# Windowed attention on one Trainium2 core: the products with v as four 64x64 quarters in two rounds

## The chip, the cores and the metric

The kernel runs on one NeuronCore of a Trainium2 chip. The metric is the device time of one execution in microseconds (us): 766.04 us for the kernel before (median of 3 runs, 765.94 to 767.62). All tensors are float32.

## What is computed

Attention over a causal window of 128 keys (8 batches, 8 heads, 576 positions, 64 wide), and behind it a maxout layer:

```python
scores = scale * np.matmul(q, k.transpose(0, 1, 3, 2))
...
mask = (rel >= 0) & (rel < window)          # rel = query - key, window = 128
scores = np.where(mask, scores + bias[None], -1000000000.0)
...
attn = attn / (np.sum(attn, axis=-1, keepdims=True) + 1e-09)
return np.matmul(attn, v).astype(np.float32)

h = np.maximum(np.maximum(x @ w1, x @ w2), x @ w3)
return (h @ w_out).astype(np.float32)
```

## The kernel before, in words

**Tasks and blocks.** A task is a batch and a pair of heads: 8 x 4 = 32 tasks. Positions are cut into five blocks of 128 (the last has 64: `rows = [128, 128, 128, 128, 64]`). A step is one block of one task; steps are handled two at a time. For each pair of steps TensorE makes the scores (`products`, L397), VectorE masks and adds the bias (L430, L444), ScalarE takes the exponential (L448) and scales (L472), TensorE transposes the result (`turn`, L481), ScalarE copies it out of PSUM (L489, L495, L498), and GpSimd masks it (L501, L505) into the tiles `pp`. A tile `pp[t, i]` has the 128 keys of block i on the partitions, and for both heads the 128 queries of block i and the 128 of block i + 1, since a key can be seen by queries up to 127 positions later.

**The products with v.** For the 28 tasks of batches 1 to 7 `mix` (L533 to L559) takes a block of 128 keys at a time: for each of the two heads one matmul with `vt[t][:n, i, j * D:(j + 1) * D]` (128 keys x 64) as the weights and the 256 query columns of `pp[t, i]` as the moving operand. The head decides the half of the array's columns and so the half of the partitions of `ps_x` (a PSUM tile of two banks, one buffer). The calls come in two groups per task: blocks 0 and 1, some steps later blocks 2, 3 and 4 (`GROUPS = (1, 4)`). The 576 output columns cross from one bank to the other at column 512, so block 3 is split there. After block 4 ScalarE copies the 576 columns to `xk` (L559). Batch 0 does the same in `mix_first` (L510 to L531), in other groups and with a copy for each. A float32 matmul of the code is two rows in the trace (28 tasks x 12 matmuls x 2 = 672).

**The maxout layer.** `plain_unit` (L722) and `unit` (L760) are 77 units per batch, in fp32r, of 6 or 9 matmuls of 128x128 weights and 288 columns; these products are made by seven products of halves instead of eight. Weights stream from DRAM into a ring of two (L314, issued by GpSimd). Results go through VectorE and ScalarE (L669 to L686, L769), and are cut into two fp32r parts for the next product (L576, L577).

**What sets the order.** Each call is an event with a due time (`at`); units are spread between the attention steps at an even pace. The recorded program is then ordered by a scheduler, up to `fix`, from which on TensorE keeps the program's order (`keep_in_program_order`, through `pe`). In the first stretch idle TensorE time is filled with dummy matmuls (`busy`, L336).

Of the kernel before, what the change touches and what calls it, by code (L numbers as in the profile page):

```python
# [29 lines left out]
def attention_maxout_kernel(  # L30
# [11 lines left out]
    nc = tc.nc  # L42
# [431 lines left out]
    def turn(s):  # L474
        pt = ps_t.tile([P, 2, 2, P], F32, name="pt")
        two = steps[s:s + 2]
        for a, (t, i) in enumerate(two):
            n = rows[i]
            p = pn.pop((t, i))
            for j in range(2):  # L480
                ins = nc.tensor.transpose(out=pt[:, a, j, :n], in_=p[:n, j], identity=ident[:n, :n])  # L481
                pe(ins)
        if idle[0] != "over":
            idle[0] = ins
            busy("t")
# [21 lines left out]
                compare_op=ALU.is_ge, fill=0.0, base=0, channel_multiplier=-1,  # L507
            )

    def mix_first(t, late):  # L510
        b, hp = tasks[t]
        x = ps_x.tile([P, 1024], F32, name="ps_x")
        c0 = FIRST * P if late else 0
        c1 = S if late else FIRST * P
        for i in range(FIRST - late, NB) if late else range(FIRST):
            n = rows[i]
            a, e = max(c0, i * P), min(c1, (i + 2) * P)
            for j in range(2):
                ins = nc.tensor.matmul(  # L519
                    x[j * D:(j + 1) * D, a - c0:e - c0],  # L520
                    lhsT=vt[t][:n, i, j * D:(j + 1) * D],
                    rhs=pp[t, i][:n, j].rearrange("p a b -> p (a b)")[:, a - i * P:e - i * P],
                    start=i == (FIRST - late if late else 0), stop=True, skip_group_check=True,
                )
                pe(ins)
        if idle[0] != "over":
            idle[0] = ins
            busy("x")
        if not late and hp % 2 == 0:
            xk[b, hp // 2] = xk_p.tile([P, 2, S], F32, name=f"xk{hp // 2}")  # L530
        nc.scalar.copy(out=xk[b, hp // 2][:, hp % 2, c0:c1], in_=x[:, :c1 - c0])  # L531

    def mix(t, i):  # L533
        b, hp = tasks[t]
        if i == 0:
            xp[t] = ps_x.tile([P, 1024], F32, name="ps_x")
        x, vv, w = xp[t], vt[t], pp[t, i]
        n = rows[i]
        m = rows[i + 1] if i + 1 < NB else 0
        parts = []  # L540
        c0 = i * P
        if m == 0 or (c0 // 512 != (c0 + P) // 512):
            parts.append((0, n, c0))
            if m:
                parts.append((P, P + m, c0 + P))
        else:
            parts.append((0, P + m, c0))
        for a, e, c in parts:
            for j in range(2):
                pe(nc.tensor.matmul(  # L550
                    x[j * D:(j + 1) * D, c:c + e - a],
                    lhsT=vv[:n, i, j * D:(j + 1) * D],
                    rhs=w[:n, j].rearrange("p a b -> p (a b)")[:, a:e],
                    start=i == 0 or (c % 512 == 0 and a == P), stop=True, skip_group_check=True,
                ))
        if i == NB - 1:
            if hp % 2 == 0:
                xk[b, hp // 2] = xk_p.tile([P, 2, S], F32, name=f"xk{hp // 2}")
            nc.scalar.copy(out=xk[b, hp // 2][:, hp % 2], in_=x[:, :S])  # L559

# [138 lines left out]
    def plain_unit(v):  # L699
# [19 lines left out]
            part_of["plain"] = ps_m.tile([P, 512], F32, name=f"ps_m{v // 2 % 3}")[:, :C]  # L719
        ps = part_of["plain"]  # L720
        for m, (lt, rt) in enumerate(pairs):
            pe(nc.tensor.matmul(  # L722
                ps, lhsT=lt, rhs=rt, start=m == 0 and c == 0, stop=m == len(pairs) - 1, skip_group_check=True,
            ))
        if (i, j, c) == (1, 1, 1):
            used.add((g, "plain"))
        if c:
# [2 lines left out]
    def unit(u):  # L730
# [26 lines left out]
            part_of[n, k] = ps_m.tile([P, 512], F32, name=f"ps_m{u % 3}")[:, :C]  # L757
        ps = part_of[n, {2: 0, 5: 0, 6: 0, 3: 1}.get(k, k)]
        for i, (lt, rt) in enumerate(pairs):
            pe(nc.tensor.matmul(  # L760
                ps, lhsT=lt, rhs=rt, start=i == 0 and k in (0, 1, 4), stop=i == len(pairs) - 1,
                skip_group_check=True,
            ))
        if g < 9:
            used.add((at, k))
        stream()
# [21 lines left out]
    for t, (b, hp) in enumerate(tasks):  # L788
        for i in range(NB):
# [27 lines left out]
                at(s + 1.3, normalise, t, i)  # L817
            if b == 0:
                if i in (FIRST - 1, NB - 1):
                    at(c + LAG_X0 + 0.001, mix_first, t, i == NB - 1)  # L820
                continue
            e = t * NB + next(min(e + 1, NB - 1) for e in GROUPS if e >= i)
            at(e - e % 2 + shift[b] + LAG_X + 0.001, mix, t, i)

    ready = [n_steps * (b + 1) - 2 + LAG_X + 0.05 + shift[b] for b in range(B)]
    ready[0] += LAG_X0 - LAG_X
# [80 lines left out]
```

## Time and profile before

| what | value |
|---|---|
| median of three runs | 766.04 us |
| span of the profiled execution | 765.8 us |
| TensorE matmul busy | 754.3 us (98%) |
| VectorE busy | 561.6 us (73%) |
| ScalarE busy | 499.6 us (65%) |
| GpSimd busy | 174.5 us (23%) |
| products with v, batches 1 to 7 (L550) | 672 matmuls, 65.3 us busy |

The profiled execution's own time is its span, 765.8 us; it lies 0.2 us under the median of the runs. PE is TensorE's matmul side, PEld its weight loads, DVE VectorE, ACT ScalarE, POOL GpSimd. A busy time is the union of the instructions' durations, and a matmul's duration runs on for a while after its last column has gone in, so a busy PE is not a full one. A group is written out<-in with its shapes (rows x columns of the array that the instruction uses, 128\*64 or 64\*64, then the output), the count, busy us and the mean ns of one.

### The profile page before, as it was taken

How to read it: one execution, taken by the hardware profiler on the slowest of the kernel's cores; microseconds unless marked ns; L12 is line 12 of the kernel's file. 1: busy time of each engine (PE TensorE's matmuls, PEld its weight loads, DVE VectorE, ACT ScalarE, POOL GpSimd, SP SyncE). 2: the span in 40 equal slices, each digit the busy share in tenths (PEclk: the TensorE clock that was granted, in tenths of full speed). 3: DMA queues.
4: the chain of work that ended last, by engine and by line, in shares of the span. 5: the costliest groups of instructions: out<-in, count | busy, mean ns of one | idle time of the engine just before them, and what ended most of it. 6: DMA issues, size and time to landing. Idle time of an engine off the chain costs nothing.

```text
span 765.8 us, 18225 instructions
## 1 busy us (share of the span) xinstructions
PE 754.3 (98%) x6417; PEld 670.4 (88%) x6417; DVE 561.6 (73%) x1921; ACT 499.6 (65%) x1674; POOL 174.5 (23%) x380
## 2 busy tenths in 40 slices
PE   9999999999999999999999999999999999999997
PEld 4588888988899998989899988999989988999987
DVE  6989997799996577947678477774769566673762
ACT  5867887687886576756677566766677566642431
POOL 2421231111141222212222122312322123311100
PEclk9999999999999999999999999999999999999999
DMA  8789975888994698737976488745887369776651
GB/s 301 262 305 320 331 266 163 293 275 298 336 308 158 197 322 281 253 128 235 318 245 213 158 299 278 260 156 204 291 292 270 106 232 307 262 225 204 226 178 63
DMA packets 56539, 187.97 MB, mean 245 GB/s; under 512 B 6144, under 2 KB 17920, under 8 KB 49664
## 3 DMA queue, kind: packets, MB, share of 16 engines
q0 software_dynamic: 16272, 99.10, 39.1%
q1 hardware_dynamic: 40032, 87.64, 33.0%
q8 instruction: 51, 0.84, 0.4%
q14 instruction: 40, 0.33, 0.1%
q10 hardware_dynamic: 144, 0.07, 0.0%
HBM read 154.53 MB, written 32.24 MB: 244 GB/s over the span
## 4 chain that ended last, share of the span: by engine, by line
PE 73%; DVE 18%; ACT 4%; DMA 2%; issue 2%; SPq 0%; POOL 0%; ACTq 0%; DVEq 0%; POOLq 0%
PE ps_m L760 48%; PE ps_x L550 6%; PE ps_m L722 6%; PE ps_s L397 6%; PE pt L481 4%; DVE hs L577 3%; PE ps_m L336 2%; DVE xs L577 2%; DVE t L683 2%; DVE s L444 2%; ACT p L448 1%; DVE hq L684 1%; DMA hs<-in_w_all 1%; DVE ps_s L430 1%; ACT xs L576 1%
## 5 line engine op out<-in xcount | busy, mean ns | idle before, releaser
L760 PE MATMUL ps_m<-xs,wt 128*128 128x288 f32 x2604 | 365.3, 298 | 3.4 <-DVE t L683 1.5
L760 PEld LDWEIGHTS ps_m<-xs,wt 128*128 128x128 f32 x2604 | 349.9, 188 | 7.2 <-DVE t L683 2.9
L448 ACT ACTIVATE p<-s,st 128x128 f32<-128x128 f32 (+1 forms) x320 | 127.0, 399 | 21.7 <-DVE st L444 21.3
L501 POOL TENSOR_SCALAR_AFFINE_SELECT pp<-pr 128x256 f32<-128x256 f32 (+1 forms) x128 | 56.8, 444 | 357.9 <-ACT pr L498 202.3
L769 ACT COPY t<-ps_m 128x288 f32<-128x288 f32 x231 | 89.5, 393 | 70.8 <-PE ps_m L760 70.1
L760 PE MATMUL ps_m<-hs,ow 128*128 128x288 f32 x882 | 124.0, 298 | 1.6 <-DVE hs L577 0.8
L760 PEld LDWEIGHTS ps_m<-hs,ow 128*128 128x128 f32 x882 | 118.7, 189 | 3.1 <-ACT t L769 1.1
L472 ACT ACTIVATE p<-p,st 128x128 f32<-128x128 f32 (+1 forms) x296 | 103.1, 396 | 21.0 <-DVE st L460 20.8
L314 POOL DMA_DIRECT2D wt<-keep x106 | 56.9, 537 | 191.7 <-PE ps_m L760 184.5
L444 DVE CUSTOM_DVE_ANT_0 s<-ps_s,bias 128x128 f32<-128x128 f32 (+1 forms) x300 | 76.3, 280 | 18.7 <-PE ps_s L397 17.0
L683 DVE TENSOR_TENSOR t<-ps_m,t 128x288 f32<-128x288 f32 x126 | 56.4, 452 | 37.2 <-PE ps_m L760 25.0
L430 DVE COPY_PREDICATED ps_s<-prev,ps_s 128x256 f32<-128x256 uint8 x120 | 50.7, 423 | 40.4 <-PE ps_s L397 39.1
L576 ACT CAST hs<-hq 128x288 fp32r<-128x288 f32 x117 | 48.9, 430 | 31.0 <-DVE hq L684 17.0
L550 PE MATMUL ps_x<-pp,v 128*64 128x256 f32 (+3 forms) x672 | 65.3, 321 | 0.0
L505 POOL TENSOR_SCALAR_AFFINE_SELECT pp<-pr 128x256 f32<-128x256 f32 (+1 forms) x128 | 63.1, 493 | 5.5 <-PE ps_x L519 5.5
L397 PE MATMUL ps_s<-qk 64*64 64x192 f32 (+1 forms) x1052 | 63.1, 323 | 0.4 <-DVE st L444 0.4
L498 ACT COPY pr<-pt 128x256 f32<-128x256 f32 x68 | 20.1, 322 | 65.7 <-PE pt L481 65.7
L448 ACT ACTIVATION_READ_ACCUMULATOR p<-s,st 128x1 f32 (+1 forms) x320 | 61.1, 191 | 0.0
L684 DVE TENSOR_TENSOR hq<-t,hq 128x288 f32<-128x288 f32 x126 | 57.0, 459 | 2.0
L577 DVE TENSOR_TENSOR hs<-hq,hs 128x288 fp32r<-128x288 f32 x117 | 53.5, 463 | 5.7 <-ACT hs L576 5.5
L550 PEld LDWEIGHTS ps_x<-pp,v 128*64 128x64 f32 (+1 forms) x672 | 38.8, 135 | 19.2 <-issue 9.1
L481 PEld LDWEIGHTS pt<-ident,p 128*128 128x128 f32 (+1 forms) x320 | 33.5, 140 | 24.1 <-issue 16.2
(84 smaller groups left out, 858.9 us busy)
## 6 DMA issues: line engine op xcount, KB each, us to landing
wt<-keep POOLq DMA_DIRECT2D x53, 1024.0 KB, 7.4
wt<-keep POOLq DMA_DIRECT2D x53, 768.0 KB, 5.8
qk<-in_qk SPq DMA_DIRECT2D x28, 576.0 KB, 5.4
hs<-in_w_all SPq DMA_DIRECT2D x20, 512.0 KB, 6.0
outT<-t SPq DMA_DIRECT2D x64, 144.0 KB, 1.8
v<-in_v SPq DMA_DIRECT2D x28, 320.0 KB, 5.3
keep<-wt SPq DMA_DIRECT2D x30, 256.0 KB, 3.7
wt<-keep SPq DMA_DIRECT2D x27, 256.0 KB, 4.2
```

Of the source, the lines that this page charges most:

```text
L397: ins = nc.tensor.matmul(ps[j][d:d + D, o:o + k1 - k0], lhsT=qkt[t][j * D:(j + 1) * D, 0, q0:q0 + D], rhs=qkt[t][j * D:(j + 1) * D, 1, k0:k1],
L444: follow(nc.vector.tensor_tensor_reduce(out=s[:n], in0=ps[j][:n, P:2 * P], in1=(bias if i else bias0)[:n, 2 * hp + j, :], scale=-0.125, sc ...
L448: nc.scalar.activation(p[:n, j], s[:n], AF.Exp, bias=st[:n, 0, a, j:j + 1], scale=-1.0, accum_out=st[:n, 1, a, j:j + 1])
L472: nc.scalar.activation(p[:n, j], p[:n, j], AF.Copy, scale=st[:n, 2, a, j:j + 1])
L481: ins = nc.tensor.transpose(out=pt[:, a, j, :n], in_=p[:n, j], identity=ident[:n, :n])
L505: nc.gpsimd.affine_select(out=w[:n, :, 0, :n], in_=r[:n, a, :, :n], pattern=[[0, 2], [1, n]], compare_op=ALU.is_ge, fill=0.0, base=0, chan ...
L550: pe(nc.tensor.matmul(x[j * D:(j + 1) * D, c:c + e - a], lhsT=vv[:n, i, j * D:(j + 1) * D], rhs=w[:n, j].rearrange("p a b -> p (a b)")[:, ...
L577: e.tensor_tensor(out=lo, in0=src, in1=hi.bitcast(F32), op=ALU.subtract)
L683: nc.vector.tensor_tensor(out=s, in0=ps, in1=e, op=ALU.add)
L684: nc.vector.tensor_tensor(out=h, in0=s, in1=h, op=ALU.max)
L760: pe(nc.tensor.matmul(ps, lhsT=lt, rhs=rt, start=i == 0 and k in (0, 1, 4), stop=i == len(pairs) - 1, skip_group_check=True,))
L769: nc.scalar.copy(out=e, in_=ps)
```

## The change

The products with v use quarters of the array: 64 keys x 64 output columns. `quarter` multiplies half r of the keys of a block by chosen query halves, for both heads. With the window of 128, half 0 of a block's keys meets the first and second half of the same block's queries and the first half of the next block's; half 1 meets the second half of the same block's and both halves of the next block's. So 6 of the 8 combinations of a key half and a query half are made, where all 8 were made before. The output of the even query halves lies in the first bank of `ps_x`, that of the odd ones in the second.

In round `near` key half 0 goes with even query halves (first bank) and key half 1 with odd ones (second bank), up to 128 columns each. In round `far` key half 0 goes with the odd half of the same block (second bank) and key half 1 with the even half of the next block (first bank), 64 columns each: the banks have swapped. Between the rounds stands the semaphore `turned`: `near` ends with `drain(fusable=True)` that raises it, and the first matmul of `far` waits for it. `far` is not issued by `mix` but held, and issued by `apart` behind the next scores, transposes or unit. In the built program 60 of the 64 raises sit on the last matmul of `near` and 4 (in batch 0) on a drain instruction of their own; 2 more drains stand ahead of transposes (`fence`). The masking and the tiles `pp` are as before. At the end of a task ScalarE copies the two banks apart, into alternating groups of 64 columns of `xk`: two copies (320 and 256 columns) instead of one of 576. `mix_first` is gone; batch 0 uses `mix` with its own bounds.

```diff
@@ products, turn, plain_unit, unit: after the last matmul
+        apart(ins)
...
+    def quarter(x, t, k, r, parts, e, first):
+        i, w = k, pp[t, k]
+        ks = slice(r * D, (r + 1) * D)
...
+        a, qs, q0 = parts
+        for j in range(2):
+            m = nc.tensor.matmul(
+                x[j * D:(j + 1) * D, q0:q0 + e * D],
+                lhsT=vt[t][ks, i, j * D:(j + 1) * D],
+                rhs=w[ks, j, a:a + e, qs * D:(qs + 1) * D],
+                start=first, stop=True, skip_group_check=True,
+            )
...
+    def turned_by():
+        ins = nc.tensor.drain(fusable=True)
...
+        ins.then_inc(turned, 1)
...
+    def near(x, t, blocks, fresh):
+        last = []
+        for n, (i, cur, nxt) in enumerate(blocks):
+            a, e = (0 if cur else 1), cur + nxt
+            last += quarter(x, t, i, 0, (a, 0, (i + a) * D), e, fresh and n == 0)
+            e = (cur and rows[i] == P) + (nxt and rows[i + 1] == P)
+            if e:
+                last += quarter(x, t, i, 1, (a, 1, 512 + (i + a) * D), e, fresh and n == 0)
+        return last
+
+    def far(x, t, blocks):
+        made = []
+        for i, cur, nxt in blocks:
+            if cur and rows[i] == P:
+                made += quarter(x, t, i, 0, (0, 1, 512 + i * D), 1, False)
+            if nxt:
+                made += quarter(x, t, i, 1, (1, 0, (i + 1) * D), 1, False)
+        return made
+
+    def apart(ins):
...
+            made = far(x, t, blocks)
+            made[0]._wait_ge(turned, turns[0])
...
+                for par in range(2):
+                    ks = [k for k in range(*done) if k % 2 == par]
+                    src = x[:, par * 512 + ks[0] // 2 * D:][:, :len(ks) * D]
+                    nc.scalar.copy(
+                        out=out[:, ks[0]:ks[-1] + 1:2], in_=src.rearrange("p (n d) -> p n d", d=D)
+                    )
...
+    def mix(t, lo, hi, first, done):
...
+        made = near(x, t, blocks[::-1] if not first else blocks, first)
...
+        made.append(turned_by())
...
+        held.append((x, t, blocks, made[-1], done))
...
-            nc.scalar.copy(out=xk[b, hp // 2][:, hp % 2], in_=x[:, :S])
```

How TensorE's rows stand, batch 1, the second group of a task. Ahead of it and behind it stand units of the maxout layer. Before:

```order
L550 MATMUL ps_x<-pp,v 64x256 [waits Pool_49]
L550 MATMUL ps_x<-pp,v 64x256
L550 MATMUL ps_x<-pp,v 64x128 [waits Pool_49]
L550 MATMUL ps_x<-pp,v 64x128
L550 MATMUL ps_x<-pp,v 64x64 [waits Pool_49]
L550 MATMUL ps_x<-pp,v 64x64
L550 MATMUL ps_x<-pp,v 64x64 [waits Pool_49]
L550 MATMUL ps_x<-pp,v 64x64
L397 MATMUL ps_s<-qk 64x128 [waits DMAHW7_49,DVE_49]
L397 MATMUL ps_s<-qk 64x128 x3
L397 MATMUL ps_s<-qk 64x192 x4
L481 MATMUL pt<-ident,p 128x128 [waits PE_49]
```

and in the changed program (L532 is the matmul of `quarter`, L482 the transpose):

```order
L532 MATMUL ps_x<-pp,v 64x64 [waits Pool_49]
L532 MATMUL ps_x<-pp,v 64x64
L532 MATMUL ps_x<-pp,v 64x128 x2
L532 MATMUL ps_x<-pp,v 64x64 x2
L532 MATMUL ps_x<-pp,v 64x128 x4
L397 MATMUL ps_s<-qk 64x128 [waits DMAHW7_49,DVE_49]
L397 MATMUL ps_s<-qk 64x128 x3
L397 MATMUL ps_s<-qk 64x192 x4
L532 MATMUL ps_x<-pp,v 64x64 [waits turned]
L532 MATMUL ps_x<-pp,v 64x64 x7
L482 MATMUL pt<-ident,p 128x128 [waits PE_49]
```

The scores, which stood behind all products with v, now stand between the two rounds; `far` stands between scores and transposes. A first group of a task stands the same way (`near` is 64x128 x8 there, `far` 64x64 x8). At four places of batches 1 to 7 there are no scores between the rounds; the last of them, at the end of batch 7, reads:

```order
L532 MATMUL ps_x<-pp,v 64x128 x4
L820 MATMUL ps_m_11222<-hs,ow_118 128x288 [waits DVE_49]
L820 MATMUL ps_m_11222<-hs,ow_118 128x288 x5
L820 MATMUL ps_m_11222<-hs_11187,ow_118 128x288 [waits DVE_49]
L820 MATMUL ps_m_11222<-hs_11187,ow_118 128x288 [waits Activation_49]
L820 MATMUL ps_m_11222<-hs_11187,ow_118 128x288
L532 MATMUL ps_x<-pp,v 64x64 [waits turned]
L532 MATMUL ps_x<-pp,v 64x64 x7
```

Here a unit of 128x128 weights has come between the two rounds, where before the products of the group stood in one piece; at the three other places it is the four transposes.

## Rows read from the trace of the kernel before

**Rows 1.** The page: span, busy time by engine (share of span, instructions), granted clock in 40 slices.
```profile
span 765.8 us, 18225 instructions
...
PE 754.3 (98%) x6417; PEld 670.4 (88%) x6417; DVE 561.6 (73%) x1921; ACT 499.6 (65%) x1674; POOL 174.5 (23%) x380
...
PEclk9999999999999999999999999999999999999999
```

**Rows 2.** Waits of PE, the largest: waited for, us in total, times, longest us.
```profile
PE ps_m L760 <- DVE t L683: 1.5, 6, 0.6
```

**Rows 3.** The chain that ended last: the page's shares by engine; its first and last L550.
```profile
PE 73%; DVE 18%; ACT 4%; DMA 2%; issue 2%; SPq 0%; POOL 0%; ACTq 0%; DVEq 0%; POOLq 0%
...
80.99 1.01 PE ps_x L550 x8
...
673.18 1.18 PE ps_x L550 x16
```

**Rows 4.** The chain that ended last, 300 to 440 us: start us, us, what.
```profile
303.87 1.01 PE ps_x L550 x8
304.88 0.81 PE ps_s L397 x16
...
308.16 0.40 ACT t L769
...
328.27 5.05 PE ps_m L760 x36
...
342.55 1.12 PE ps_x L550 x14
...
351.26 1.01 PE ps_x L550 x8
```

**Rows 5.** Timeline of PE, a second group (493 us), and scores without a group (70 us).
```profile
493.35 1.19 PE L550 MATMUL ps_x<-pp,v 128*64 128x256 f32 x14
...
494.37 0.23 PE L550 MATMUL ps_x<-pp,v 64*64 64x64 f32 x2
...
495.06 0.66 PE L481 MATMUL pt<-ident,p 128*128 128x128 f32 x4
...
70.25 0.76 PE L397 MATMUL ps_s<-qk 64*64 64x192 f32 x12
70.94 0.66 PE L481 MATMUL pt<-ident,p 128*128 128x128 f32 x4
```

**Rows 6.** Groups with shapes kept apart: xcount | busy us, mean ns | idle before.
```profile
L550 PE MATMUL ps_x<-pp,v 128*64 128x256 f32 x336 | 48.7, 396 | 0.0
...
L550 PE MATMUL ps_x<-pp,v 128*64 128x128 f32 x112 | 10.9, 273 | 0.0
...
L550 PE MATMUL ps_x<-pp,v 128*64 128x64 f32 x112 | 8.0, 220 | 0.0
```

**Rows 7.** L550, then L397 from 303 to 306 us: ns min/median/max; L397 from 304.80 to 304.84.
```profile
L550 PE MATMUL ps_x<-pp,v x8: 379/380/431, 303.8 to 304.5; 128*64 128x256 f32 x8
...
L397 PE MATMUL ps_s<-qk x16: 322/323/374, 304.8 to 305.4; 64*64 64x192 f32 x16
...
304.81 0.39 PE L397 MATMUL ps_s<-qk 64*64 64x192 f32 x4
```

**Rows 8.** ScalarE: the copy of one task on the timeline, and by form (as rows 6).
```profile
494.64 0.64 ACT L559 COPY xk<-ps_x 128x576 f32<-128x576 f32 x1
...
L769 ACT COPY t<-ps_m 128x288 f32<-128x288 f32 x231 | 89.5, 393 | 70.8 <-PE ps_m L760 70.1
```

**Rows 9.** Stretches: us, busy us of PE, PEld, DVE, ACT, POOL, clock, DMA share, GB/s.
```profile
80.00:100.00 20.00, 20.00 (x184) 16.72 (x184) 19.82 (x69) 15.89 (x58) 4.47 (x10) 1.00 0.98 341
100.00:120.00 20.00, 19.65 (x188) 17.30 (x185) 19.77 (x72) 17.41 (x63) 4.08 (x8) 1.00 0.65 221
...
398.00:418.00 20.00, 20.00 (x177) 18.99 (x176) 19.12 (x57) 15.15 (x46) 5.33 (x11) 1.00 0.68 235
```

**Rows 10.** Timeline of PE at 292.5 us: idle time just before, and what ended it.
```profile
292.50 0.53 PE L760 MATMUL ps_m<-xs,wt 128*128 128x288 f32 x2 [0.19 <-DVE t L683]
```

More of the change, by code (lines that the diff above doesn't have):

```diff
@@ L482, in turn @@
                 pe(ins)
+                if not fixed and fence[0] is not None and fence[1] is None:
+                    after(ins, fence[0])
+                    fence[1] = ins
+        apart(ins)
         if idle[0] != "over":
@@ L508, in turn @@
             )
[L510 to L525, printed above, removed]
+    held = []
@@ new lines, in attention_maxout_kernel, with after @@
+    turned = tc.alloc_semaphore("turned")
+    turns = [0]
+    fence = [None, None]
+    def after(ins, first):
+        tc.add_manual_dep(
+            ins.ins, first.ins.name,
+            mybir.DependencyInfo(mybir.DependencyClass.NoSync, mybir.DependencyReason.DATA), reason="order",
+        )
+    def quarter(x, t, k, r, parts, e, first):
+        i, w = k, pp[t, k]
+        ks = slice(r * D, (r + 1) * D)
+        ins = []
+        a, qs, q0 = parts
[6 more added lines that the diff above has]
+            )
+            pe(m)
+            ins.append(m)
+        return ins
@@ new lines, in far @@
+    def far(x, t, blocks):
[7 more added lines that the diff above has]
+    def apart(ins):
+        while held:
+            x, t, blocks, last, done = held.pop(0)
+            if not fixed:
+                after(ins, last)
+            made = far(x, t, blocks)
+            made[0]._wait_ge(turned, turns[0])
+            fence[:] = [None if fixed else made[-1], None]
+            if not fixed:
+                after(made[0], ins)
+                for m, n in zip(made[1:], made):
+                    after(m, n)
+            if done is not None:
+                b, hp = tasks[t]
+                if hp % 2 == 0 and (b, hp // 2) not in xk:
+                    xk[b, hp // 2] = xk_p.tile([P, 2, S], F32, name=f"xk{hp // 2}")
+                out = xk[b, hp // 2][:, hp % 2].rearrange("p (n d) -> p n d", d=D)
+                for par in range(2):
[3 more added lines that the diff above has]
+                        out=out[:, ks[0]:ks[-1] + 1:2], in_=src.rearrange("p (n d) -> p n d", d=D)
+                    )
@@ new lines, in mix @@
+    def mix(t, lo, hi, first, done):
+        if first:
+            xp[t] = ps_x.tile([P, 1024], F32, name="ps_x")
+        x = xp[t]
+        blocks = []
+        for i in range(NB):
+            cur = lo <= i < hi
+            nxt = lo <= i + 1 < hi if tasks[t][0] == 0 else cur and i + 1 < NB
+            if cur or nxt:
+                blocks.append((i, cur, nxt))
+        made = near(x, t, blocks[::-1] if not first else blocks, first)
+        if fence[0] is not None:
+            if fence[1] is None:
+                fence[1] = nc.tensor.drain()
+                after(fence[1], fence[0])
+            after(made[0], fence[1])
+        made.append(turned_by())
+        if not fixed:
+            for m, n in zip(made[1:], made):
+                after(m, n)
@@ L526, in mix_first @@
         if idle[0] != "over":
-            idle[0] = ins
+            idle[0] = made[-1]
             busy("x")
[L529 to L558, printed above, removed]
-            nc.scalar.copy(out=xk[b, hp // 2][:, hp % 2], in_=x[:, :S])
@@ L819, in attention_maxout_kernel @@
                 if i in (FIRST - 1, NB - 1):
-                    at(c + LAG_X0 + 0.001, mix_first, t, i == NB - 1)
+                    late = i == NB - 1
+                    at(
+                        c + LAG_X0 + 0.001, mix, t, FIRST if late else 0, NB if late else FIRST, True,
+                        (2 * FIRST, 9) if late else (0, 2 * FIRST),
+                    )
                 continue
-            e = t * NB + next(min(e + 1, NB - 1) for e in GROUPS if e >= i)
-            at(e - e % 2 + shift[b] + LAG_X + 0.001, mix, t, i)
+            if i in GROUPS:
+                e = t * NB + min(i + 1, NB - 1)
+                lo = GROUPS[0] + 1 if i == NB - 1 else 0
+                at(e - e % 2 + shift[b] + LAG_X + 0.001, mix, t, lo, i + 1, lo == 0, (0, 9) if i == NB - 1 else None)
     ready = [n_steps * (b + 1) - 2 + LAG_X + 0.05 + shift[b] for b in range(B)]
```

15 lines of the change are left out of this document (11 added, 4 removed).

## The prediction, written before the changed kernel ran

> **What bounds the kernel now.** I read the page first. PE is busy for 754.3 of 765.8 us and the granted clock stands at full speed in every slice [rows 1], so the clock is no part of this change. A busy PE need not be the bound; PE's waits tell whether it is. The longest, for VectorE's L683, comes to 1.5 us in the whole span [rows 2]: PE hardly ever waits. The chain that ended last says the same from the other side: 73% of it is PE [rows 3]. The second thing to see is where that chain leaves PE. In a stretch of 90 us it runs through units, products with v (L550), scores and transposes, leaves PE at 308.16 us and comes back at 328.27 us [rows 4]; in between ScalarE and VectorE set the pace, and time that PE saves there is lost. So what counts is not all of L550 but what of it is on this chain: 46 pieces, the first at 81.0 and the last at 673.2 us [rows 3], of the 56 that 28 tasks make. 25 of them are first groups of 1.01 us and 21 second groups, 18 of 1.12 us and 3 of 1.18 us [rows 3, 4]: 49 us.
>
> **What a column costs.** The rows of L550 by form differ in columns alone: 128 columns last 273 ns and 64 last 220 ns, so 64 columns are 53 ns [rows 6]; 256 columns have a median of 380 ns [rows 7], so 128 more are 107 ns. That is 0.83 ns for a column and a row of the trace. Eight rows of 256 columns take 1.01 us [rows 4]. One after another they would need 8 x 0.213 = 1.70 us; with the two heads side by side 4 x 0.213 = 0.85 us. So the two halves of the array run together, and 0.16 us is left for going into and out of this shape. The scores show the same for quarters: 16 rows of 64x192 take 0.81 us [rows 4], where two at a time would need 8 x 0.16 = 1.28 us and four at a time need 0.64 us. Scores are laid out as the change lays out its quarters: the half of the rows decides the bank, the half of the columns the partitions, and both halves of the columns take moving operands of their own. So I take four quarters to run together in `near` and `far` too.
>
> **The first group of a task.** Before: 1.01 us. After: `near` has two blocks of 128 columns in each quarter, each in two passes: 4 x 0.107 = 0.43 us. `far` has 4 passes of 64 columns, which the trace shows in halves of the array but not in quarters. From below a pass costs its columns, 0.053 us, with its weight load under the pass before. From above, a load not hidden costs as much as the first of a group shows, 431 against 380 ns [rows 7]: 0.051 us, so 0.104 us a pass. I take the lower, 0.21 us for `far`, since the rows of 64 columns, with as short a pass to hide a load under, are 53 ns shorter than those of 128 and not the same [rows 6]. The scores now stand in the same shape as both rounds, so the 0.16 us is saved as well. Gain: 1.01 - 0.43 - 0.21 = **0.37 us**.
>
> **The second group.** Before: from its start at 493.35 to the transposes at 495.06 are 1.71 us, scores of 12 rows included; scores of 12 rows alone take from 70.25 to 70.94, 0.69 us [rows 5]. So the group costs 1.02 us (1.12 us on the chain, since its last block runs beside the scores). After: the rows of the array that hold key half 0 have the longer way, 64 + 128 + 128 columns in two passes, 0.53 us; `far` again 0.21 us. Gain: **0.27 us**. The other half of the rows idles 0.21 us meanwhile, which I give no value.
>
> **The wait for `turned`.** It is new on PE. The semaphore sits on the last matmul of `near` and needs that matmul's end, not just its last column: 273 - 107 = 0.17 us more, and the next engine starts 0.04 us later still (ScalarE's copy starts at 494.64, PE's last row ends at 494.60 [rows 5, 8]). Behind the waiting matmul stand the rest of `far`, the transposes and the next units. But between the rounds now stand 0.5 to 0.65 us of scores, so the wait is over when PE gets there: nothing. Without that cover it would cost 0.2 us for each group, 64 times 0.2 = 13 us, about the whole gain. At four places no scores stand there but transposes or a unit; these cover the wait too, but the array changes its shape twice more. At the 0.16 us found above for once, I give these (117.44, 657.58, 664.94 and 673.18 us) a gain of 0.1 us in all. The drains of batch 0 lie where I count no gain.
>
> **The other engines.** ScalarE: 576 columns took 0.64 us; 320 and 256 columns cost about twice the 0.39 us of 288 [rows 8], 0.14 us more for a task, under 5 us in all on an engine that is busy 65% [rows 1]; they stand ahead of the copies of the transposes on ScalarE, as before, and `far` ends before the transposes do. If ScalarE became the bound, those 5 us would come off the gain. The copies end later than before by the scores and `far`, about 0.8 us; the next task's `near`, which needs the single `ps_x`, comes 8 us after the second group (342.55 and 351.26 [rows 4]). GpSimd and the loads keep their order and move with PE.
>
> **Sum.** 24 first groups x 0.37 = 8.9, 18 second groups x 0.27 = 4.9, the four places 0.1: 13.9 us. From this I take off two things. Between 80 and 120 us VectorE is busy for 39.59 of 40 us [rows 9], so the two full gains there (0.64 us) mostly meet a full VectorE: 0.5 us off. And what is late next: in each batch there are places where PE already waits for VectorE, 0.19 us at 292.5 [rows 10], and 20 us in which VectorE is busy for 19.12 [rows 9]; a PE that arrives earlier waits there. There are some five such batches; I take off 1.9 us, 0.3 to 0.4 us each, an estimate from these rows, as no row gives it. Left are 11.5 us. The profiled execution has a span of 765.8 us and stands 0.2 us under the median, so from 766.0 I come to **754.5 us**. In batch 0 I count nothing: its groups lie in dummy matmuls or under a full VectorE.
>
> **Rivals.**
> *Nothing is lost on the way.* PE waits for nothing new and groups off the chain help as well: 28 x 0.37 + 28 x 0.27 = 17.9 us, 748 us. For it speaks that VectorE idles 27% [rows 1]; against it the 20 us off PE in each batch [rows 4].
> *Short passes cost double.* If a load does not hide under 64 columns, `far` takes 0.42 us; the gains fall to 0.16 and 0.06 us, 24 x 0.16 + 18 x 0.06 = 4.9 us, less the same discounts in proportion: 4 us, 762 us. A fixed price for each matmul would do the same. Against both speak the 53 ns above, and four rows of L397 that start within 0.04 us [rows 7]. The Trainium skill (TensorEngine Tiling (Array Packing), Instruction Overhead) gives each matmul about 60 cycles, which would be 25 ns, and warns against tiling a dimension that is already small. By that page the 16 rows of `far` would need 0.40 us, and the sum would be this rival's; the four starts within 0.04 us speak against it in quarters.
> *The halves of the keys take turns (slower).* If the two halves of the rows do not run together when they add into the same tile in two rounds, a first group takes 2 x (0.43 + 0.21) = 1.28 us instead of 1.01, a second 0.53 + 0.32 + 0.43 = 1.28 instead of 1.02: 46 x 0.265 = 12 us more, 778 us. It decides from where the rounds take over 1.01 / 0.64 = 1.6 times the time of four together. Against it speak the scores at 0.81 us.
> *Others absorb it (no change).* If VectorE's chain binds all through, less than 2.3 us are left, 764 to 766 us. PE's 1.5 us of waiting speaks against it.
>
> **How the numbers follow.** Within 0.3% means within 2.3 us, about what a measurement of this kernel can tell from no change. Chances: the forecast, 751 to 758.5 us, 0.60; nothing lost 0.13; double price 0.14, nearly all of it faster by over 2.3 us; absorbed 0.06; slower 0.07. That gives faster 0.86, same 0.07, slower 0.07. The range of 748.5 to 763.0 us takes in the double price and leaves out the best of the first rival and the last two, under 2 in 10.
>
> **What would show it.** In the profile of the changed kernel L532 should have 28 x 68 rows in batches 1 to 7, all 64\*64; from the start of a first group's `near` to the scores 0.4 to 0.5 us; from the end of the scores to the transposes 0.2 us more than now; no wait of PE on itself ahead of `far`. PE's waits for VectorE should grow to 2 or 4 us. A `near` of 0.8 us would mean halves in turn, a `far` of 0.4 us short passes at double price; PE waits of 10 us would mean that the gain was absorbed. Unknown in the sum are the order that the scheduler gives batches 0 and 1, and any price of a moving operand of two pieces of 64 columns, which no row shows.

## The result, and the profile after

The changed kernel is slower: 776.64 us (median of 4 runs, 775.92 to 776.99) against 766.56 us for the kernel before beside it (4 runs, 765.94 to 767.62). The ratio on record is 1.0122, 95% interval 1.0104 to 1.0141 (the two medians alone would give 1.0131). The prediction of 754.5 us, and its range of 748.5 to 763.0 us, were wrong, and wrong in sign. An execution's recorded time lies 1.7 to 2.1 us above its span (776.99 and 775.3 us for the profiled one here), so spans are compared with spans below; by that the profiled execution of before, with 765.8 us, took some 767.6 us, above its median and not 0.2 us under it.

The head of the page of the changed kernel, against [rows 1]: TensorE is busy 10 us less, the granted clock is the same (90% or more in every slice, 0.998 over the span), and the span is 9.5 us longer.

```profile
span 775.3 us, 21134 instructions
...
PE 743.9 (96%) x7851; PEld 688.3 (89%) x7857; DVE 564.8 (73%) x1921; ACT 499.2 (64%) x1710; POOL 174.4 (22%) x380
...
PEclk9999999999999999999999999999999999999999
```

So work went and time came. Did the quarters do what they should? The timeline of TensorE around the first group of a task in batch 3 of the changed kernel (start, length, line, operation, shapes, count):

```profile
361.94 0.29 PE L820 MATMUL ps_m<-xs,wt 128*128 128x288 f32 x1
362.16 0.67 PE L532 MATMUL ps_x<-pp,v 64*64 64x128 f32 x16
362.65 0.83 PE L397 MATMUL ps_s<-qk 64*64 64x192 f32 x16
363.30 0.41 PE L532 MATMUL ps_x<-pp,v 64*64 64x64 f32 x16
363.64 0.70 PE L482 MATMUL pt<-ident,p 128*128 128x128 f32 x4
364.27 0.40 PE L820 MATMUL ps_m<-xs,wt 128*128 128x288 f32 x1
```

They did. `near` takes 0.49 us from its first start to the scores', `far` 0.34 us, and no idle time stands ahead of `far`: the wait for `turned` is covered. Single rows come in fours that start within 0.02 us, the next four 109 ns later in `near` (128 columns; 160 ns after the very first four) and 58 ns later in `far` (64 columns). From the start of the last unit row ahead of such a block to that of the first one behind it, a block with 16 scores took 2681 ns before and takes 2335 ns (median of 12), one with a second group 2360 and 2111 ns: **0.35 and 0.25 us saved**, where 0.37 and 0.27 were forecast.

The waits of TensorE show where time came from (what it waited for, us in all, times, longest). Before, the list began with 1.5 us for VectorE's L683 [rows 2] and summed to 7.6 us; now it sums to 27.3 us and begins:

```profile
PE ps_m L820 <- ACT t L831: 5.6, 11, 0.8
PE ps_s L397 <- DVE st L445: 4.5, 5, 1.5
PE ps_m L820 <- DVE hs L635: 2.9, 5, 0.8
PE ps_m L780 <- DVE xs L635: 2.1, 2, 1.2
PE ps_m L820 <- DVE t L741: 2.0, 3, 1.3
PE ps_m L820 <- DMA wt<-keep: 1.8, 1, 1.8
```

The chain that ended last says the same: TensorE has 57% of it instead of 73% [rows 3], VectorE 23% instead of 18%, DMA 6% instead of 2%.

```profile
PE 57%; DVE 23%; issue 7%; DMA 6%; ACT 5%; SPq 1%; POOL 1%; DVEq 0%; POOLq 0%; ACTq 0%
```

**Where along the run.** Every kernel of this case has the same 576 rows of `plain_unit` and 3,528 rows of `unit`, in the same order. The start of a given row in one trace, less its start in another, is what has been lost up to there. The table gives it against the kernel before, for the changed kernel and for those that follow (their names say which batches have quarters; `_ord` holds engines to the order of before, except that before_ord has that of q2to7 and before_oq0 that of q0). Single profiles differ by about 1 us here: up to 153 us q2to7, q2to7_ord and before_ord do what before does, and stand at -1.1 to +1.1. A profile is one execution; that of q0 is the slowest of its four, 3 us over their median.

| row starts before at | 39.1 | 77.1 | 119.0 | 152.6 | 249.8 | 628.4 | 762.2 us |
|---|---|---|---|---|---|---|---|
| changed kernel | +2.3 | +4.3 | +7.3 | +7.1 | +11.9 | +8.1 | +9.6 |
| q2to7 | +1.1 | +0.4 | +0.6 | +0.6 | +4.9 | +1.6 | +0.4 |
| q0 | +3.0 | +6.8 | +6.6 | +6.6 | +7.2 | +8.1 | +7.9 |
| q1 | +0.3 | -0.1 | +3.6 | +3.5 | +3.4 | +4.4 | +4.7 |
| q2to7_ord | +0.4 | -1.1 | -0.8 | -0.8 | -0.6 | -8.3 | -6.3 |
| before_ord | +1.1 | +0.7 | +0.7 | +0.7 | +5.9 | +10.5 | +10.7 |
| q1to7_ord | +0.8 | -0.5 | -0.2 | -0.5 | 0.0 | -7.2 | -6.6 |
| after_ord | +4.1 | +7.8 | +8.5 | +8.2 | +8.4 | +0.1 | +0.9 |
| q0_ord | +3.0 | +6.7 | +7.1 | +7.1 | +6.8 | +7.7 | +6.5 |
| before_oq0 | +0.2 | +5.4 | +5.3 | +5.3 | +5.0 | +5.9 | +6.3 |
| q0_direct_ord | +0.8 | +0.3 | +0.5 | +0.5 | +0.2 | +1.6 | +0.7 |
| before_two | +0.5 | -0.6 | -0.6 | -0.6 | -0.2 | +0.6 | -0.5 |

The changed kernel loses in three places, 4.3 us up to 77 us (batch 0), 3 us up to 119 us (batch 1), 4.8 us between 153 and 250 us (batch 2), wins back 3.8 us over the next five batches, and loses 1.5 us at the end. Eight groups a batch save 8 x 0.3 = 2.4 us of TensorE's time; only 0.8 us a batch arrive.

### The profile page after: what moved, and what is told of

It is laid out like the page before. It is cut to its first block, busy times and chain, and to the rows that moved or that the text cites. A ratio compares the mean times of both kernels' runs of the same rounds, so it can differ in the third digit from the quotient of the medians.

```text
span 775.3 us, 21134 instructions
## 1 busy us (share of the span) xinstructions
PE 743.9 (96%) x7851; PEld 688.3 (89%) x7857; DVE 564.8 (73%) x1921; ACT 499.2 (64%) x1710; POOL 174.4 (22%) x380
## 4 chain that ended last, share of the span: by engine, by line
PE 57%; DVE 23%; issue 7%; DMA 6%; ACT 5%; SPq 1%; POOL 1%; DVEq 0%; POOLq 0%; ACTq 0%
PE ps_m L820 42%; PE ps_x L532 4%; PE ps_s L397 4%; PE ps_m L780 4%; PE pt L482 4%; DVE hs L635 3%; DVE s L445 2%; DMA wt<-keep 2%; ACT p L449 2%; DVE t L741 2%; DVE hq L742 2%; DMA hs<-in_w_all 2%; DVE ps_s L431 1%; DVE wt L160 1%; DVE xt L148 1%
## 5 line engine op out<-in xcount | busy, mean ns | idle before, releaser
L820 PE MATMUL ps_m<-xs,wt 128*128 128x288 f32 x2604 | 368.8, 298 | 9.1 <-ACT t L831 3.0
L532 PE MATMUL ps_x<-pp,v 64*64 64x64 f32 (+1 forms) x2056 | 78.3, 249 | 0.3 <-PE ps_m L780 0.3
L532 PEld LDWEIGHTS ps_x<-pp,v 64*64 64x64 f32 x2056 | 58.7, 132 | 12.6 <-issue 11.5
L397 PE MATMUL ps_s<-qk 64*64 64x192 f32 (+1 forms) x1052 | 61.8, 316 | 4.3 <-DVE st L445 4.1
L482 PE MATMUL pt<-ident,p 128*128 128x128 f32 (+1 forms) x320 | 54.5, 281 | 3.1 <-DVE p L468 1.2
L635 DVE TENSOR_TENSOR hs<-hq,hs 128x288 fp32r<-128x288 f32 x117 | 51.3, 452 | 8.3 <-ACT hs L634 7.5
L780 PE MATMUL ps_m<-xs,wt 128*128 128x288 f32 x336 | 49.4, 300 | 2.4 <-DVE xs L635 2.1
```

Source lines behind the costliest of these rows:

```text
L397: ins = nc.tensor.matmul(ps[j][d:d + D, o:o + k1 - k0], lhsT=qkt[t][j * D:(j + 1) * D, 0, q0:q0 + D], rhs=qkt[t][j * D:(j + 1) * D, 1, k0:k1],
L532: m = nc.tensor.matmul(x[j * D:(j + 1) * D, q0:q0 + e * D], lhsT=vt[t][ks, i, j * D:(j + 1) * D], rhs=w[ks, j, a:a + e, qs * D:(qs + 1) * ...
L635: e.tensor_tensor(out=lo, in0=src, in1=hi.bitcast(F32), op=ALU.subtract)
L780: ins = nc.tensor.matmul(ps, lhsT=lt, rhs=rt, start=m == 0 and c == 0, stop=m == len(pairs) - 1, skip_group_check=True,)
L820: ins = nc.tensor.matmul(ps, lhsT=lt, rhs=rt, start=i == 0 and k in (0, 1, 4), stop=i == len(pairs) - 1, skip_group_check=True,)
```

## Experiments

A ratio below is the one on record of a kernel to the kernel before, run beside it, with its 95% interval. The kernel before stood at 768.2 to 769.1 us then; the expectations in us take 766 for it, so a ratio times 766 is to be held against them.

### 1. Which batches lose

**Theory A**: the loss comes with the order that the scheduler gives the engines, the quarters gain. **Theory B**: the saved time is absorbed by VectorE and ScalarE, wherever the quarters stand. Three kernels have the quarters in some batches only; the other batches have the old `mix_first` and `mix` back (`mix_whole`). In q2to7 these are batches 2 to 7, in q0 batch 0, in q1 batch 1.

```diff
+QUARTERS = (2, 3, 4, 5, 6, 7)
...
+                    if b not in QUARTERS:
+                        at(c + LAG_X0 + 0.001, mix_first, t, late)
+                        continue
...
+            if b not in QUARTERS:
+                e = t * NB + next(min(e + 1, NB - 1) for e in GROUPS if e >= i)
+                at(e - e % 2 + shift[b] + LAG_X + 0.001, mix_whole, t, i)
+                continue
```

> Quarters in batches 2 to 7 alone; batches 0 and 1 have the products of the kernel before, and so, up to about 250 us, the order of before on every engine. Theory A (the loss comes from the stretch that the scheduler orders, the quarters themselves gain): the trace of the changed kernel goes from 11.9 us behind at 250 us to 7.1 us behind at 712 us and 9.6 us behind at the end, so here the same stretch gives 4.8 us of gain at 712 us and 2 to 5 us at the end: 761 to 764 us. Theory B (the quarters cost by themselves, wherever they stand: the new waits for ScalarE and VectorE of about 0.5 us per task): no gain in batches 2 to 7, 766 us or more. Theory C (what is lost up front is only lent, and the later part just makes it up because there is slack after a delay): no gain here either, 766 us.

Measured: 0.9991 of before (0.9977 to 1.0004): no gain from 48 groups. Theories B and C said so; A, with the loss only in the stretch where the scheduler orders TensorE too, missed.

> Quarters in batch 0 alone (8 groups, with the 6 drains); everything from batch 1 on is as before. Theory A: the loss of batch 0 is here, 7 us behind at 120 us as in the changed kernel, and what of it stays at the end is 3 to 7 us: 769 to 773 us. Theory B: batch 0 has only 8 of 64 groups, under 2 us of loss: 766 to 768 us.

Measured: 1.0064 (1.0041 to 1.0087), as theory A had it. By the table nearly all of it is lost up to 77 us.

> Quarters in batch 1 alone. In the changed kernel the stretch from 170 to 250 us loses 4.7 us. Theory A (the order that the scheduler gives batch 1): the loss appears here too, 3 to 5 us, 769 to 771 us. Rival D (batch 1 loses only because batch 0 came late, its waits follow from that): the quarters gain 1 to 2 us here, 764 to 766 us.

Measured: 1.0062 (1.0043 to 1.0081): rival D falls. The loss is not where it was expected: it lies between 77 and 119 us, and from 153 to 250 us, where batch 2 stands, q1 loses nothing. Between 77 and 119 us TensorE's scores wait for VectorE's work on earlier ones. The waits there, before, in q1 and in q1to7_ord (section 3), whose VectorE has the order of before:

```profile
PE ps_s L397 <- DVE st L444: 0.4, 1, 0.4
```

```profile
PE ps_s L398 <- DVE st L446: 3.6, 4, 1.8
```

```profile
PE ps_s L405 <- DVE st L453: 1.4, 3, 0.6
```

In the changed kernel it is 4.1 us of the 4.5 in the list above.

The three together, 0.64 + 0.62 - 0.09 = 1.17%, are the changed kernel's 1.22%, within the intervals. So the causes lie in the batches themselves. q2to7 looks like theory B or C. But `fix`, from the first group of batch 2 on, at 157 us of before, pins TensorE's order only. VectorE, ScalarE, SyncE and GpSimd are ordered by the scheduler to the end, and it orders them by what it takes each instruction to last, TensorE's included (no run here varies those durations). In the built programs VectorE's list of q2to7 differs from that of before by 416 lines of difference (in the changed kernel by 631, in q0 by 203, in q1 by 96), up to the last batch, though VectorE has the same 1,921 rows in the trace; ScalarE's rows are rearranged as much (428 lines in q2to7, some 70 of them for the added copies), GpSimd's hardly (2 lines). So A and B had to be told apart by crossing work and order.

### 2. Work and order crossed

q2to7_ord has the work of q2to7, before_ord that of the kernel before; each is given the other's order on the four engines by edges that fix the order of issue and are no waits of their own:

```diff
+ORDER = {
+    'DVE': [106, 108, ...
...
+    made = {i.name: i for i in nc.cur_bb.bb.instructions}
+    for names in ORDER.values():
+        for a, b in zip(names, names[1:]):
+            tc.add_manual_dep(
+                made[f"I-{b}"], f"I-{a}",
+                mybir.DependencyInfo(mybir.DependencyClass.NoSync, mybir.DependencyReason.DATA), reason="order",
+            )
```

> Quarters in batches 2 to 7 as in q2to7, but VectorE, ScalarE, GpSimd and SyncE are held to the order that the scheduler gave them in the kernel before (the two copies of a task stand where the one copy stood, except for the last task). q2to7 lost 4.3 us between 170 and 250 us and then came back by 0.9 us per batch, where 2.4 us of TensorE's time per batch are gone. Theory A1 (the rearranged order on the other engines costs, there and in every later batch): the loss at 170 to 250 us is gone and the later batches give up to 2 us each: 754 to 760 us. Theory B (the saved time is absorbed by VectorE or ScalarE whatever their order): 764 to 767 us.

Measured: **0.9906** (0.9889 to 0.9923), 7.2 us of 766 faster than before.

> The crossed case: the products of the kernel before in every batch, TensorE's order as before, but VectorE, ScalarE, GpSimd and SyncE held to the order that the scheduler gave them in q2to7. No work is changed at all. Theory A1: the order alone costs: 4 us or more lost between 170 and 250 us, 770 to 776 us. Theory B: the order is harmless: 765 to 767 us.

Measured: **1.0121** (1.0101 to 1.0141), 9.3 us slower, with no work changed. Its page counts 6417 matmul rows, as before [rows 1]; in the traces TensorE's rows stand in the order of before and VectorE's in that of q2to7.

| | order of before | order of q2to7 |
|---|---|---|
| work of before | 1 | 1.0121 |
| quarters in batches 2 to 7 | 0.9906 | 0.9991 |

The quarters gain in either order, and the order costs with either work: theory A holds, with the order of the other engines behind `fix` counted in, and B falls. C falls too: q2to7_ord has no delay at 250 us and wins 7.7 us up to 628 us, and before_ord, 5.9 us late at 250 us, makes up nothing. q2to7 was no null result but two opposite ones.

How does an order cost? The waits of TensorE from 160 to 250 us, first before, then q2to7 (its L793 is L683 of before, L161 is L160):

```profile
PE ps_m L760 <- ACT t L769: 0.6, 1, 0.6
PE ps_m L760 <- DVE st L460: 0.4, 1, 0.4
```

```profile
PE ps_m L872 <- DVE t L793: 2.2, 3, 1.4
PE ps_m L872 <- DVE wt L161: 1.0, 2, 0.7
PE ps_m L872 <- ACT t L883: 0.7, 1, 0.7
PE ps_m L872 <- DVE hq L788: 0.7, 1, 0.7
PE ps_m L872 <- DVE hq L796: 0.7, 2, 0.4
```

That is 5.3 us against 1.0, and the 4.3 us more are what q2to7 loses between 153 and 250 us in the table. The longest stands at 180.71 us in TensorE's timeline of q2to7; in before the same row starts at 177.98 us without a wait.

```profile
178.71 0.56 PE L872 MATMUL ps_m<-xs,wt 128*128 128x288 f32 x3
180.71 1.45 PE L872 MATMUL ps_m<-xs,wt 128*128 128x288 f32 x9 [1.45 <-DVE t L793]
```

VectorE's timeline ahead of it, before:

```profile
172.41 0.44 DVE L683 TENSOR_TENSOR t<-ps_m,t 128x288 f32<-128x288 f32 x1
172.88 0.46 DVE L684 TENSOR_TENSOR hq<-t,hq 128x288 f32<-128x288 f32 x1
173.26 0.45 DVE L683 TENSOR_TENSOR t<-ps_m,t 128x288 f32<-128x288 f32 x1
...
174.38 0.95 DVE L160 TENSOR_TENSOR wt<-hs,wt 128x768 fp32r<-128x768 f32 x1
...
177.14 0.44 DVE L683 TENSOR_TENSOR t<-ps_m,t 128x288 f32<-128x288 f32 x1
```

and in q2to7:

```profile
173.60 0.96 DVE L161 TENSOR_TENSOR wt<-hs,wt 128x768 fp32r<-128x768 f32 x1 [0.47 <-ACT wt L160]
175.09 0.42 DVE L216 TENSOR_TENSOR hs<-hs 128x256 f32<-128x256 f32 x1 [0.53 <-DMA hs<-w]
175.44 0.45 DVE L793 TENSOR_TENSOR t<-ps_m,t 128x288 f32<-128x288 f32 x1
...
176.50 0.45 DVE L793 TENSOR_TENSOR t<-ps_m,t 128x288 f32<-128x288 f32 x1
...
180.21 0.44 DVE L793 TENSOR_TENSOR t<-ps_m,t 128x288 f32<-128x288 f32 x1
```

Before, VectorE frees two of the units' PSUM banks (L683) and then cuts the 768 columns of weights (L160). In q2to7 the cut of the weights stands first. It waits 0.47 us for ScalarE's half of it, the next row 0.53 us for a transfer, and both L793 stand behind. VectorE is busy 16.66 of 16.8 us in this stretch of before (169.5 to 186.3 us), so an idle microsecond there is not made up, and TensorE waits for the third L793. The Trainium skill (PSUM — Partial Sum Buffer, Engine vs sequencer instructions) says that the queues of VectorE, ScalarE and GpSimd are strictly first in, first out; these rows agree: VectorE's rows start in the order of its list, and both L793 start only behind the two waits of 0.47 and 0.53 us.

### 3. Batches 0 and 1, and the whole change

**Theory E**: in batches 0 and 1, ahead of `fix`, the order edges that the change itself puts on TensorE cost as well. The table ORDER is added to the changed kernel (after_ord), to quarters in batches 1 to 7 (q1to7_ord) and in batch 0 alone (q0_ord). Ahead of `fix` TensorE is left to the scheduler in after_ord and q0_ord; in q1to7_ord a key `'PE'` of the table holds it to the order that the scheduler gives it with these quarters and no table. before_oq0 is the kernel before with the other engines in q0's order.

> The changed kernel whole, quarters in all batches, with VectorE, ScalarE, GpSimd and SyncE held to the order of the kernel before; TensorE's order is left to the scheduler, with the order edges of the change. q2to7_ord stood at 0.9906 of before. Theory A1 (the order on the other engines is the whole loss): batches 0 and 1 add nothing or a little: 754 to 762 us where before is 766. Theory E (in batch 0 and 1 the order edges that the change puts on TensorE, near ahead of the scores, far and fences behind, cost by themselves): 3 to 7 us more, 763 to 768 us.

Measured: 1.0003 (0.9988 to 1.0017), 766 us, in theory E's range. The order of the other four engines is not the whole loss.

> Quarters in batches 1 to 7, the other engines held to the order of the kernel before, TensorE's order as the scheduler gave it with quarters. Theory A1: as q2to7_ord, with up to 0.6 us more or less from batch 1, where VectorE is full: 757 to 760 us where before is 766. Theory E: batch 1 loses 3 us: 761 to 763 us.

Measured: 0.9924 (0.9902 to 0.9947), 760.2 us, between the two ranges and nearer to theory A1's: batch 1 loses nothing against before (-0.2 us at 119 us in the table), though TensorE has the scheduler's order there.

> Quarters in batch 0 alone (q0 stood at 1.0064 of before), the other engines held to the order of the kernel before. Theory A1: the loss is gone, 765 to 767 us. Theory E: it stays, 769 to 773 us, since TensorE's own edges are all there.

Measured: 1.0094 (1.0071 to 1.0117), as theory E had it. Theory A1 falls for batch 0.

> The products of the kernel before in all batches, but VectorE, ScalarE, GpSimd and SyncE held to the order that they had in q0; TensorE is free of the change's edges. Theory A1: the order alone costs 4 to 7 us: 770 to 773 us. Theory E: 765 to 768 us.

Measured: 1.0066 (1.0043 to 1.0090). By the expectations this is theory A1, and q0_ord is theory E: in batch 0 the loss comes either way. q0_ord has the others in the old order and still loses 0.94%, where q0_direct_ord below, with TensorE in the old order too, loses 0.23%: TensorE's order costs by itself. before_oq0 is less clean: TensorE, free up to `fix`, took an order of its own there (145 lines of difference from before, up to 106 us), so what the other engines' order costs alone in batch 0 is not shown. TensorE's waits from 10 to 80 us, all of before's and the first of q0_ord's:

```profile
PE ps_m L722 <- DVE xs L577: 0.8, 1, 0.8
PE ps_m L722 <- ACT ow L159: 0.4, 1, 0.4
```

```profile
PE pt L489 <- ACT p L456: 1.0, 1, 1.0
PE ps_m L404 <- DVE st L452: 0.8, 1, 0.8
```

Before has no wait there for the attention's own steps. The wait of 1.0 us stands at the same place in the changed kernel. TensorE's timeline there, before:

```profile
21.68 1.30 PE L519 MATMUL ps_x<-pp,v 128*64 128x256 f32 x12
22.91 0.64 PE L397 MATMUL ps_m<-xs 64*64 64x256 f32 x2
23.49 0.66 PE L481 MATMUL pt<-ident,p 128*128 128x128 f32 x4
```

and in the changed kernel:

```profile
21.41 0.65 PE L397 MATMUL ps_m<-xs 64*64 64x256 f32 x4
23.08 0.41 PE L482 MATMUL pt<-ident,p 128*128 128x128 f32 x2 [1.02 <-ACT p L449]
...
24.58 0.72 PE L532 MATMUL ps_x<-pp,v 64*64 64x128 f32 x19
```

The products of a group stood ahead of the transposes and covered ScalarE's exponentials; now most of them stand behind, and the transposes wait with nothing to cover them.

Two more kernels tell edges from order in batch 0. In q0_direct `far` stands directly behind `near`, with the drain between them, and nothing pins scores or transposes; in q0_direct_ord all engines, TensorE too, are in the order of before, both rounds at the place of the old products.

```diff
         held.append((x, t, blocks, made[-1], done))
+        if b == 0:
+            apart(None)
...
-                if not fixed and fence[0] is not None and fence[1] is None:
-                    after(ins, fence[0])
-                    fence[1] = ins
```

> Quarters in batch 0 alone, but near and far stand directly behind each other with a drain between them, at the place of the old products, and all engines, TensorE too, are held to the order of the kernel before; no edge pins scores or transposes to the rounds. q0 stood at 1.0064, q0_ord (other engines in the old order, TensorE with the change's edges) at 1.0094. Theory E (TensorE's order in batch 0, with its edges from near to scores to far and from far to transposes, is what costs there): the loss is gone, 765 to 768 us where before is 766, the drains costing up to 1.6 us. Rival F (the two rounds hold the single ps_x longer, so the next group and ScalarE's copy come late whatever the order): 3 us or more are still lost, 769 us or more.

Measured: 1.0023 (1.0009 to 1.0037), 767.8 us, in theory E's range: rival F falls.

> As q0_direct_ord, near and far directly behind each other with a drain and without edges on scores and transposes, but every engine's order is left to the scheduler. Theory E in its narrow form (the edges alone): 765 to 768 us. If the scheduler's own choice of order costs, edges or no: 769 to 773 us, as q0.

Measured: 1.0083 (1.0062 to 1.0105).

Without the edges but in the scheduler's order the loss stays; in the old order 1.8 us of it are left (0.7 to 2.8). That is about what the drains were given, but no run shows that it is the drains: the table has this kernel only 0.3 us behind at 77 us. So theory E's narrow form falls: in batch 0 too it is the order, here TensorE's as well as the others'.

### 4. The added copies, and which engine's order

A rival for the steady part: the second copy on ScalarE.

```diff
-            nc.scalar.copy(out=xk[b, hp // 2][:, hp % 2], in_=x[:, :S])
+            for cs in (slice(0, 5 * D), slice(5 * D, S)):
+                nc.scalar.copy(out=xk[b, hp // 2][:, hp % 2, cs], in_=x[:, cs])
```

> The kernel before with one change: the copy of 576 columns is made as two, of 320 and 256 columns; the order of TensorE, GpSimd and SyncE is that of before to the row, VectorE's almost. Tests a rival for the steady part, that the 28 added ScalarE copies (0.14 us each, 4 us of ScalarE) are what takes the gain: then 768 to 770 us. If ScalarE hides them: 765.5 to 767 us.

Measured: 1.0001 (0.9981 to 1.0020). Two copies in place of one cost nothing that shows. They write plain columns here, in the changed kernel alternating groups of 64; ScalarE's means are the same (424 and 377 ns here, 420 and 375 ns there).

Then q2to7 with VectorE, with ScalarE, and with SyncE and GpSimd in the old order (those keys of ORDER alone), and the whole change with all engines in it. The engines that are not held are the scheduler's, and it rearranges them again.

> q2to7 (0.9991 of before) with VectorE alone held to the order of the kernel before; all engines held gave 0.9906. If VectorE's order carries the loss: 0.990 to 0.994. If ScalarE's or the loads': 0.997 to 1.001.

Measured: 0.9919 (0.9891 to 0.9947).

> q2to7 with ScalarE alone held to the order of the kernel before. If ScalarE's order carries the loss: 0.990 to 0.994; if VectorE's: 0.997 to 1.001, or above 1.001, as the two orders no longer fit together.

Measured: 0.9973 (0.9957 to 0.9989).

> q2to7 with SyncE's and GpSimd's orders alone, the loads and stores and the masks, held to those of the kernel before. If the loads' order carries the loss: 0.990 to 0.994; if not: 0.997 to 1.001.

Measured: 0.9985 (0.9969 to 1.0001).

VectorE in the old order is enough in batches 2 to 7: it gives back 0.7 of the 0.85% that all four give, though ScalarE then stands in a third order (254 lines of difference from q2to7, 304 from before). The loads' order matters by nothing that shows. What ScalarE's order is worth with VectorE as in q2to7 is not shown: 0.9973 lies at the edge of what was expected if VectorE's carries the loss, but with ScalarE held VectorE took a third order too (388 lines from q2to7, 428 from before). That kernel stands 9.3 us behind before at 250 us and wins 11.0 us up to 628 us, where q2to7_ord wins 7.7. The late start alone hardly explains that (after_ord, 8.4 us late there in the old order, wins 8.3), so another order may serve the later batches better than that of before; no run separates the two.

> The whole change, quarters in all eight batches; in batch 0 near and far stand together with a drain between; all engines, TensorE too, follow the order of the kernel before. If the order is the whole of the loss: q1to7_ord's 0.9924 and what q0_direct_ord lost (1.0023) together, 0.992 to 0.995, 760 to 763 us where before is 766. If the quarters of batches 0 and 1 to 7 disturb each other: 0.996 or more.

Measured: **0.9937** (0.9914 to 0.9959). That is 761.2 us, as expected if the order is the whole of the loss. The whole change in the old order beats the kernel before by about 4.8 us, and is 1.8% faster than the change as the scheduler ordered it. The lowest ratio of all is q2to7_ord's 0.9906; its interval overlaps with that of this kernel.

## Why the prediction was wrong

**Right: the quarters.** Four run together, 58 ns for 64 columns where 53 were taken, and the short passes do not cost double. By the rule of the Trainium skill that the prediction weighed (TensorEngine Tiling (Array Packing), Instruction Overhead) the 16 rows of `far` would, by the prediction's estimate, have needed 0.40 us. Four passes of 58 ns are 0.23 us, so the trace does not agree with adding that price up over quarters that run together. The halves do not take turns: `near` takes 0.49 us, not 0.8. The 0.16 us for the change of shape were placed wrongly, which hardly moved the sum: `near` takes 0.06 us more than its columns, `far` 0.34 us to the transposes, 0.11 us more than its passes, and in return the scores, which took 0.81 us to the transposes [rows 4], now take 0.65 us.

**Right: what was costed at nothing.** From batch 2 on TensorE has no idle time ahead of `far`, and the copies cost nothing that shows (before_two).

**Right in the steady part, once the order is kept.** The sum gave 13.9 us over seven batches, 2.0 us each, less 0.3 to 0.4 us of new waits. In q2to7_ord the five batches from 250 to 628 us give 7.7 us, 1.5 us each (7.2 us in q1to7_ord, 8.3 us in after_ord). The new waits are there. TensorE's waits from 250 to 660 us, before and then in q2to7_ord:

```profile
PE ps_m L760 <- DVE t L683: 1.5, 6, 0.6
```

```profile
PE ps_m L878 <- DVE t L799: 1.9, 6, 0.9
PE ps_m L878 <- ACT t L889: 1.4, 4, 0.4
PE ps_m L878 <- DVE hq L800: 0.3, 2, 0.2
```

That is 2.1 us more, 0.4 us a batch, as estimated. They need not come with the quarters: in q2to7_act TensorE waits 0.4 us in the same stretch and 2.2 us a batch arrive.

**Too small: the discount for a full VectorE.** It was taken for 80 to 120 us alone, 0.5 us. Batch 2 meets a VectorE as full, 16.66 of 16.8 us, and gains nothing (-0.8 to -0.6 us); batch 1 gains nothing either (q1to7_ord, -0.2 us). That is some 3 us. And 2 us are given back behind the attention, where TensorE, now early, waits for VectorE and the weights (-8.3 to -6.3 us): the sum had no term for it. With these, taken from the same traces after the fact, the sum would be 6 to 7 us, near the 7.2 us of q2to7_ord, and 759 us, inside the range.

**Wrong: that the order stays.** The step that failed is the order of the other engines, put at nothing without a reason. The prediction says "GpSimd and the loads keep their order and move with PE" and takes the same for VectorE and ScalarE without saying it; with it stands "In batch 0 I count nothing". What it says of GpSimd is so, and the loads' order shows no cost (q2to7_dma); what it left unsaid is what failed. The prediction named the order of batches 0 and 1 as unknown at its end, but gave it no bound and no chance, and took the batches behind `fix` as safe. `fix` holds TensorE alone. The rearranged lists of the other engines cost 9.3 us with the old work (before_ord), and in batches 0 and 1, where TensorE's list is the scheduler's too, 0.64 and 0.62% more. The 0.07 for slower lay on another mechanism, the halves in turn. One of the prediction's signs was met and misleads: waits of TensorE of 10 us "would mean that the gain was absorbed". They came to 27.3 us, but where the order is kept the gain arrives. That 631 lines of VectorE's order differ could be read in the built program beforehand; which way it would go could not, and a bound from both sides would have made the range hold both signs.

Left open: which of the scheduler's assumed durations tips it, since no run changed them; what ScalarE's order is worth alone; and what the last 1.8 us of batch 0 are.

## What to carry to other kernels

Where a scheduler orders the engines, a change on one engine is a change on all of them: compare the built order of every engine, and where it moves, give the order a term of its own, with both signs. To learn what an edit is worth, cross it with the order: old work in the new order, new work in the old. A result of "no difference" can be a gain and a loss of the same size, and the order of the old kernel can be kept by hand to have most of the gain. An engine that is not held is ordered anew, so look at the order of every engine in each such kernel before reading it as the effect of one.

## What had not been expected of the hardware

Rows in quarters do not start strictly one behind the other. In a second group the half of the array that has less to do goes on to the scores while the other still works at `near`: two rows of L397 start ahead of the last two of L532, which stand ahead of them in TensorE's list. The timeline of the changed kernel:

```profile
353.70 0.66 PE L532 MATMUL ps_x<-pp,v 64*64 64x64 f32 x18
354.15 0.28 PE L397 MATMUL ps_s<-qk 64*64 64x128 f32 x2
354.20 0.28 PE L532 MATMUL ps_x<-pp,v 64*64 64x128 f32 x2
354.26 0.76 PE L397 MATMUL ps_s<-qk 64*64 64x128 f32 x14
```

So the 0.21 us that the prediction left idle in the shorter half are partly filled by the scores; what that is worth is not shown, as the group saves 0.25 us and not more than forecast.

It bears on `turned` too. The raise sits on the last matmul of `near` in TensorE's list, and in a second group that one belongs to the shorter half. In all 28 second groups of batches 1 to 7 four rows of `near` start behind the row that carries the raise (here it starts at 354.05, the last at 354.21 us), and by the trace, in which the ends of matmuls are modelled, `near` ends 0.16 us after that row. So there `turned` does not stand for the end of `near`; the work between the rounds covers that as well.
